# Attention and two feed-forward layers on one core: feed-forward units of one tile take two 128-blocks of the hidden layer at a time, and the order of all work is drawn anew

## The chip, the cores and the metric

The kernel runs on one core of one Trainium2 chip. The metric is the device time of one execution in microseconds, the median of several runs. TensorE has two parts in the profile, PE (matmuls) and PEld (weight loads); VectorE is DVE, ScalarE is ACT, GpSimd is POOL, and SyncE is SP, which issues the DMAs.

## The reference

Attention over 4 x 8 heads with 576 rows of 64 columns, in which each row keeps its 32 largest scores; the result, seen as 2304 tokens by 512 columns, goes through two feed-forward layers with a hidden width of 2048.

```python
scores = scale * np.matmul(q, k.transpose(0, 1, 3, 2))
kth = np.partition(scores, -top_k, axis=-1)[..., -top_k:-top_k + 1]
scores = np.where(scores >= kth, scores, -1000000000.0)
attn = np.exp(scores - np.max(scores, axis=-1, keepdims=True))
attn = attn / (np.sum(attn, axis=-1, keepdims=True) + 1e-09)
x = np.matmul(attn, v)            # then to (B * S, H * D)
x = (s * np.maximum(x @ w_in, 0.0) ** 2 + b) @ w_out      # first layer
x = np.maximum(x @ w2_in, 0.0) ** 2 @ w2_out              # second layer
```

## The kernel before

The 2304 tokens are 18 tiles of 128 (tiles 4 and 13 hold the last 64 rows of two batches). For each tile and each of its 8 heads PE makes the scores (line L599), DVE finds the 32 largest with four MAX8 and three MATCH_REPLACE8 over 576 columns (L610, L621) and writes the masked exponentials (L652 for tiles 0 to 11, L658 after that), ACT computes the exponential and a 16-bit copy (L624, L654, L661), POOL the remainder of that copy (L456), a DMA transposes both, and PE multiplies with the values (L685, 15 matmuls a head; twice as many in tiles 4 and 13). Every operand is held as a high and a low half in 16 bits, so each product takes three matmuls.

The weights come as 64-bit words. DVE, ACT and POOL convert them to 32 bits in 64 pieces (L919, L928, L935 on DVE), PE finds a scale (L980), and each piece is split into halves. W0 and W1 are the first layer's two matrices, W2 and W3 the second's.

The feed-forward work is cut into units, of one tile or of two. The first layer has 12 units of one tile (the first eleven and the last) and 3 of two; the second layer has 2 of one tile (the first and the last) and 8 of two. A unit goes through 16 blocks `f` of 128 hidden columns. For each block PE makes the hidden values in PSUM (`f_in`, 12 matmuls, L788), ACT applies ReLU (L797, out `rr`), squares it once in 16 bits (L799, `gh`) and once in 32 (L802, `gg` or `sqr`), POOL takes the difference (L807, `gl`), and PE multiplies `gh` and `gl` with the second matrix (`f_out`, 3 matmuls for each tile, L834, into the bank `pC0` or `pC1`). In a unit of two tiles all of this is 256 columns wide and the hidden values stand in the bank `pH`. In a unit of one tile it is 128 wide, and every other block uses the bank `pC1` in place of `pH` once the later weights are there:

```python
pin, pn_ = (pC[1], "pC1") if nt == 1 and h2 and rdy else (pH, "pH")
```

The order is not that of the code. `Plan.add` records each operation with its engine, a cost in us, what it reads and writes, and a priority; `Plan.order` simulates the five engines with these costs and takes, whenever an engine is free, the ready operation of lowest priority. The table `TW` adds a number to the priority, one for each group of operations (`A3.1` is tile 3, heads 2 and 3; `F04` the first layer's unit 4) and one for each step (`pe4` is `f_in`, `pe5` is `f_out`). Each engine then runs its list in that fixed order and waits at each instruction for what it needs.

Of the kernel before, what the change touches and what calls it, by code (L numbers as in the profile page):

```python
# [9 lines left out]
F16 = mybir.dt.float16  # L10
# [40 lines left out]
LASTW = 1  # L51
# [22 lines left out]
    "A0.0": -0.8, "A0.1": 19.1, "A0.2": 49.0, "A0.3": -60.0, "A1.0": 4.6, "A1.1": -6.1, "A1.2": 10.3, "A1.3": -41.3,  # L74
    "A10.0": -52.1, "A10.1": 25.4, "A10.2": 2.3, "A10.3": 0.9, "A11.0": -30.1, "A11.1": -10.9, "A11.2": 58.3,
    "A11.3": 35.8, "A12.0": 32.1, "A12.1": 45.1, "A12.2": -13.9, "A12.3": -8.8, "A13.0": -23.0, "A13.1": 59.7,
    "A13.2": 25.9, "A13.3": 2.1, "A14.0": 53.9, "A14.1": -15.9, "A14.2": 53.3, "A14.3": 57.6, "A15.0": 46.3,
    "A15.1": 1.8, "A15.2": 24.4, "A15.3": 30.8, "A16.0": -28.7, "A16.1": 46.6, "A16.2": 36.9, "A16.3": 51.2,
    "A17.0": 58.1, "A17.1": -8.9, "A17.2": 53.4, "A17.3": -50.4, "A2.0": 1.0, "A2.1": 49.3, "A2.2": -18.2,
    "A2.3": 22.0, "A3.0": 27.2, "A3.1": -35.9, "A3.2": -60.0, "A3.3": 48.1, "A4.0": 54.4, "A4.1": -60.0,  # L80
    "A4.2": -29.6, "A4.3": 35.7, "A5.0": -59.0, "A5.1": -57.6, "A5.2": -2.7, "A5.3": 23.9, "A6.0": -8.9,
    "A6.1": 58.2, "A6.2": 55.2, "A6.3": -60.0, "A7.0": -17.8, "A7.1": -22.1, "A7.2": -19.5, "A7.3": -44.5,
    "A8.0": 19.5, "A8.1": 6.1, "A8.2": -56.7, "A8.3": 60.0, "A9.0": -36.6, "A9.1": -20.3, "A9.2": 49.4,
    "A9.3": -44.4, "CS": 13.0, "E00": 14.4, "E01": 39.8, "E010": 60.2, "E011": -18.4, "E012": 9.3, "E013": -10.9,
    "E014": 1.1, "E02": 24.1, "E03": -60.0, "E04": -47.3, "E05": -52.7, "E06": -58.2, "E07": 58.5, "E08": 6.8,
# [1104 lines left out]
```

## Time and profile before

| | |
|---|---|
| three runs | 1160.61, 1156.14, 1159.86 us; median 1159.86 |
| profiled execution, first to last instruction | 1163.6 us |
| mean granted TensorE clock in it | 0.982 |
| HBM read, written | 89.65 MB, 8.91 MB |

The profiled execution is one more run of the same program, and its span is 3.7 us longer than the median of the three. A busy time in the profile is the sum of an engine's instructions; those of PE are modelled to the end of the pipeline and overlap one another, so the distance from one start to the next tells what a matmul costs.

### The profile page before, as it was taken

The page shows a single profiled execution, that of the slowest core. Times are in us where ns is not written, and L with a number is a line of the kernel's source. Part 1 is how long each engine was busy: PE and PEld are TensorE (multiplying, and loading weights), DVE is VectorE, ACT ScalarE, POOL GpSimd, SP SyncE. Part 2 cuts the span into 40 slices and gives each one's busy share as a digit, 9 for nine tenths or more (in the row PEclk, how much of TensorE's full clock was granted, in tenths as well). Part 3 has the DMA queues.
Part 4 walks back from the last instruction along what each step waited for, and adds up shares of the span by engine and source line. Part 5 has one row for each costly group of instructions (what it writes and reads, how often), then busy time and mean ns, then how long its engine had stood idle before and what let it go on. Part 6 is the DMA issues. An engine that isn't in the chain of part 4 may idle for free. (4 is left out here: it accounts for less than half of the span.)

```text
span 1163.6 us, 27825 instructions
## 1 busy us (share of the span) xinstructions
PE 1033.9 (89%) x10052; PEld 693.2 (60%) x10052; DVE 954.7 (82%) x2034; ACT 884.4 (76%) x2354; POOL 677.5 (58%) x1109
## 2 busy tenths in 40 slices
PE   1476867689989999999999999999999999999998
PEld 1232344356667667666666776666666666666665
DVE  6999999999988999999999999987999999500000
ACT  3488869879889878879987899768777686564645
POOL 4676359766667756656775577646654474452322
PEclk9988989899999999999999999999999999999999
DMA  8888974676976774687588656765376277223530
GB/s 258 243 230 199 233 193 114 181 203 138 212 124 143 151 178 84 112 189 163 98 152 183 138 104 114 172 156 118 76 178 147 53 133 181 47 64 118 172 100 29
DMA packets 338219, 171.17 MB, mean 147 GB/s; under 512 B 292512, under 2 KB 317088, under 8 KB 338080
## 3 DMA queue, kind: packets, MB, share of 16 engines
q1 hardware_dynamic: 338080, 169.39, 62.9%
q8 instruction: 78, 1.28, 0.5%
q14 instruction: 61, 0.50, 0.2%
HBM read 89.65 MB, written 8.91 MB: 85 GB/s over the span
## 5 line engine op out<-in xcount | busy, mean ns | idle before, releaser
L788 PEld LDWEIGHTS <-w 128*128 128x128 f16 x4800 | 364.6, 98 | 87.7 <-issue 23.1
L788 PE MATMUL pH<-xT,w 128*128 128x256 f16 (+1 forms) x3648 | 368.2, 251 | 12.5 <-ACT rr L797 10.5
L456 POOL TENSOR_TENSOR pn<-et,pn 128x576 f16<-128x576 f32 x144 | 185.9, 1293 | 57.6 <-ACT pn L654 24.8
L797 ACT ACTIVATE rr<-pH,rsc 128x256 f32<-128x256 f32 (+1 forms) x304 | 128.8, 424 | 109.0 <-PE pH L788 107.0
L807 POOL TENSOR_TENSOR gl<-gg,gh 128x128 f16<-128x128 f32 (+1 forms) x216 | 114.4, 530 | 141.3 <-ACT gg L802 53.0
L610 DVE MAX8 m<-wk 128x8 f32<-128x576 f32 x252 | 188.9, 749 | 1.2
L834 PE MATMUL pC<-wo,gh 128*128 128x512 f16 x576 | 171.4, 379 | 0.0
L807 POOL TENSOR_TENSOR gl<-sqr,gh 128x128 f16<-128x128 f32 (+1 forms) x184 | 100.2, 545 | 115.6 <-ACT sqr L802 53.5
L834 PE MATMUL pC<-wring,gh 128*128 128x512 f16 x544 | 161.8, 379 | 1.7 <-DMA wring<-wo 1.1
L799 ACT ACTIVATE gh<-rr 128x128 f16<-128x128 f32 (+1 forms) x400 | 139.6, 352 | 8.2 <-PE pC L834 3.0
L834 PEld LDWEIGHTS <-gh 128*128 128x128 f16 x1152 | 103.0, 98 | 68.9 <-issue 2.3
L610 DVE MAX8 m<-spare 128x8 f32<-128x576 f32 x180 | 135.0, 750 | 0.6
L624 ACT ACTIVATE et<-pS,ngm,cq 128x576 f32<-128x576 f32 x144 | 119.0, 826 | 14.7 <-DVE wk L621 3.9
L621 DVE MATCH_REPLACE8 wk<-m,wk 128x576 f32<-128x576 f32 x168 | 124.8, 743 | 0.0
L610 DVE MAX8 m<-pS 128x8 f32<-128x576 f32 x144 | 108.2, 756 | 19.1 <-PE pS L599 18.7
L685 PEld LDWEIGHTS <-pT 128*128 128x128 f16 (+1 forms) x2400 | 85.8, 102 | 44.5 <-DMA pT<-pn 29.9
L834 PE MATMUL pC<-wo,gl 128*128 128x512 f16 x288 | 109.2, 379 | 2.8 <-POOL gl L807 2.8
L685 PE MATMUL pA<-vp,pT 128*128 128x64 f16 (+1 forms) x2400 | 95.0, 196 | 16.5 <-DMA pT<-pn 15.4
L834 PE MATMUL pC<-wring,gl 128*128 128x512 f16 x272 | 103.1, 379 | 0.0
L834 PEld LDWEIGHTS <-gl 128*128 128x128 f16 x576 | 56.3, 98 | 72.9 <-POOL gl L807 5.8
L599 PE MATMUL pS<-kT,qT 128*128 128x512 f16 (+2 forms) x320 | 84.4, 298 | 12.6 <-DVE et L652 10.3
L621 DVE MATCH_REPLACE8 spare<-m,spare 128x576 f32<-128x576 f32 x120 | 89.2, 743 | 0.0
(208 smaller groups left out, 1796.4 us busy)
## 6 DMA issues: line engine op xcount, KB each, us to landing
wring<-wo SPq DMA_DIRECT2D x72, 512.0 KB, 3.9
wring<-in_moe_w_out_dram SPq DMA_DIRECT2D x18, 512.0 KB, 3.8
wring<-in_moe_w_in_dram SPq DMA_DIRECT2D x17, 512.0 KB, 4.6
xT<-in_moe_w_in_dram SPq DMA_DIRECT2D x15, 512.0 KB, 5.8
xT<-in_moe_w_out_dram SPq DMA_DIRECT2D x14, 512.0 KB, 4.3
qW<-qT SPq DMA_DIRECT2D x36, 128.0 KB, 2.4
kvraw<-in_k_dram SPq DMA_DIRECT2D x16, 256.0 KB, 3.6
kvraw<-in_v_dram SPq DMA_DIRECT2D x16, 256.0 KB, 3.2
```

Of the source, the lines that this page charges most:

```text
L456: add(pool, step, c_pool(cols * (c.stop - c.start) / n), prio, lambda c=c: nc.gpsimd.tensor_tensor(o[:, c], x[:, c], y[:, c], op=op), r=r, ...
L599: nc.tensor.matmul(s[r0:r0 + n, c0:c0 + cn_], lhsT=w[:, h, r0:r0 + n], rhs=kk[:, k0:k0 + cn_], start=(a == 0), stop=(a == 1))
L610: add(dve, "dv10", 0.67, prio, lambda src=src, rd=rd: nc.vector.max(m[:, 8 * rd:8 * rd + 8], src), r=[sn], w=[f"m{i2}_{rd}"])
L621: add(dve, "dv11", 0.735, prio, lambda src=src, rd=rd: nc.vector.match_replace(wk, m[:, 8 * rd:8 * rd + 8], src, NEG), r=[sn, f"m{i2}_{rd} ...
L624: add(act, "ac9", 0.72, prio, lambda: nc.scalar.activation(out=e, in_=s, func=ACTF.Exp, bias=ngm[i2][:, 0:1], scale=cq[q2][:, j:j + 1]), r ...
L685: nc.tensor.matmul(pA[r0:r0 + n, h, :], lhsT=pT[p3][:, a * 5 + c, r0:r0 + n], rhs=vv[:, vc, z, :], start=(c == 0 and a == 0 and z == 0), s ...
L788: nc.tensor.matmul(ps_, lhsT=win[:, f, a, kk, :], rhs=x[:, z * KD + kk, :], start=(kk == 0 and a == 0 and z == 0), stop=(kk == KD - 1 and ...
L797: add(act, "ac18", 0.14 + n / 1200.0, prio, lambda r=r, pin=pin, rs=rs: nc.scalar.activation(out=r, in_=pin[:, 0:n], func=ACTF.Relu, scale ...
L799: add(act, "ac19", 0.094 + n / 1200.0, prio, lambda r=r, hi=hi: nc.scalar.activation(out=hi, in_=r, func=ACTF.Square), r=rrn, w=ghn)
L807: add(pool, "po19", 0.12 + n * 0.0021, prio, lambda gt=gt, hi=hi, lo=lo: nc.gpsimd.tensor_tensor(lo, gt, hi, op=ALU.subtract), r=gn + ghn, ...
L834: nc.tensor.matmul(pC[tt], lhsT=src[g3][:, c], rhs=wt(a), start=(f == 0 and a == 0 and src is gh), stop=(f == KF - 1 and src is gl))
```

## The change

A unit of one tile now takes two blocks in one step (`nf = 2`). The 24 first matmuls of a step write both halves of the first 256 columns of `pH`; ReLU, both squares and the difference are one instruction each, 256 wide; six second matmuls follow. `pC1` no longer holds hidden values. Units of two tiles are computed as before. In the 14 units of one tile, 224 steps become 112, with the same matmuls. All numbers of `TW` are new, so the order of everything else changes too.

```diff
-    "A0.0": -0.8, "A0.1": 19.1, "A0.2": 49.0, "A0.3": -60.0, "A1.0": 4.6, "A1.1": -6.1, "A1.2": 10.3, "A1.3": -41.3,
+    "A0.0": -13.0, "A0.1": 32.7, "A0.2": 66.3, "A0.3": 39.0, "A1.0": -56.0, "A1.1": -21.8, "A1.2": 55.4, "A1.3": -3.9,
...
-        for f in range(KF):
+        n, nf = 256, 2 // nt
+        for f in range(0, KF, nf):
...
-            parts = "ab" if nt == 2 else "ab"[nsub[0] // 2 % 2]
-            part3 = "ab" if nt == 2 else "ab"[nsub[0] // 3 % 2]
-            if nt == 1:
-                h2, g3 = nsub[0] % 2, nsub[0] % 3
-                g1 = h2 if rdy else 0
-                nsub[0] += 1
...
-            pin, pn_ = (pC[1], "pC1") if nt == 1 and h2 and rdy else (pH, "pH")
-
-            def f_in(f=f, pin=pin):
-                ps_ = pin[:, 0:n]
-                for kk in range(KD):
-                    for a, z in ((0, 0), (0, 1), (1, 0)):
-                        nc.tensor.matmul(ps_, lhsT=win[:, f, a, kk, :], rhs=x[:, z * KD + kk, :],
-                                         start=(kk == 0 and a == 0 and z == 0),
-                                         stop=(kk == KD - 1 and a == 1))
-
-            add(pe, "pe4", 12 * max(PEN, 0.0022 + n / 2400.0), prio, f_in,
-                r=rx + [f"{wname}h{f}", f"{wname}l{f}"], w=[pn_])
+            fs = range(f, f + nf)
+
+            def f_in(fs=fs):
+                for j, ff in enumerate(fs):
+                    ps_ = pH[:, j * nt * 128:(j + 1) * nt * 128]
+                    for kk in range(KD):
+                        for a, z in ((0, 0), (0, 1), (1, 0)):
+                            nc.tensor.matmul(ps_, lhsT=win[:, ff, a, kk, :], rhs=x[:, z * KD + kk, :],
+                                             start=(kk == 0 and a == 0 and z == 0),
+                                             stop=(kk == KD - 1 and a == 1))
+
+            add(pe, "pe4", 12 * nf * (0.0022 + 128 * nt / 2400.0), prio, f_in,
+                r=rx + [f"{wname}{z}{ff}" for ff in fs for z in "hl"], w=["pH"])
...
-            add(act, "ac18", 0.14 + n / 1200.0, prio, lambda r=r, pin=pin, rs=rs: nc.scalar.activation(
-                out=r, in_=pin[:, 0:n], func=ACTF.Relu, scale=rs), r=[pn_, f"rsc{which}"], w=rrn)
+            add(act, "ac18", 0.14 + n / 1200.0, prio, lambda r=r, rs=rs: nc.scalar.activation(
+                out=r, in_=pH[:, 0:n], func=ACTF.Relu, scale=rs), r=["pH", f"rsc{which}"], w=rrn)
...
-            def f_out(f=f, g3=g3, wt=wt, o3=o3):
-                for tt in range(nt):
-                    c = slice(o3 + tt * 128, o3 + tt * 128 + 128)
+            def f_out(fs=fs, g3=g3, wt=wt):
+                for j, (ff, tt) in enumerate([(ff, tt) for ff in fs for tt in range(nt)]):
+                    c = slice(j * 128, j * 128 + 128)
                     for src, a in ((gh, 0), (gh, 1), (gl, 0)):
-                        nc.tensor.matmul(pC[tt], lhsT=src[g3][:, c], rhs=wt(a),
-                                         start=(f == 0 and a == 0 and src is gh),
-                                         stop=(f == KF - 1 and src is gl))
-
-            add(pe, "pe5", nt * 0.65, prio + 1.2, f_out, r=ghn + gln + rw,
+                        nc.tensor.matmul(pC[tt], lhsT=src[g3][:, c], rhs=wt(a, ff),
+                                         start=(ff == 0 and a == 0 and src is gh),
+                                         stop=(ff == KF - 1 and src is gl))
+
+            add(pe, "pe5", 1.3, prio + 1.2, f_out, r=[*ghn, *gln, *rw],
                 w=[f"pC{tt}" for tt in range(nt)])
```

What moves shows best on three engines. The number behind a name in the rows is that of a buffer; `pC_189` is `pC0`, `pC_190` is `pC1`, `w_67` and `w_68` are weights. In the changed file the lines stand up to 14 higher: L599 is now L598, L685 is L684, L788 is L776, L797, L799 and L802 are L784, L786 and L789, L807 is L794, L834 is L820.

First ACT, in the last unit of the second layer, a unit of one tile. Before, three instructions of 128 columns for each block, with the sources `pH` and `pC1`:

```order
L797 ACTIVATE rr_111<-pH,rsc_182 128x128
L802 ACTIVATE gg<-rr_111 128x128
L797 ACTIVATE rr_112<-pC_190,rsc_182 128x128
L802 ACTIVATE sqr<-rr_112 128x128
L799 ACTIVATE gh_114<-rr_112 128x128
L799 ACTIVATE gh_115<-rr_111 128x128
L797 ACTIVATE rr_112<-pC_190,rsc_182 128x128
L802 ACTIVATE sqr<-rr_112 128x128
L799 ACTIVATE gh_116<-rr_112 128x128
```

In the changed kernel, three of 256 columns for two blocks:

```order
L784 ACTIVATE rr_112<-pH,rsc_182 128x256
L789 ACTIVATE sqr<-rr_112 128x256
L786 ACTIVATE gh_114<-rr_112 128x256
L784 ACTIVATE rr_111<-pH,rsc_182 128x256
L789 ACTIVATE gg<-rr_111 128x256
L786 ACTIVATE gh_115<-rr_111 128x256
L784 ACTIVATE rr_112<-pH,rsc_182 128x256
L789 ACTIVATE sqr<-rr_112 128x256
L786 ACTIVATE gh_116<-rr_112 128x256
```

Nine instructions now cover six blocks where nine covered three, ReLU reads `pH` each time, and squares and ReLU alternate in a fixed turn.

Second PE, in the same unit, at the passage from a second matmul to the next first one. Before (each row with what it waits for):

```order
L834 LDWEIGHTS gh_116
L834 MATMUL pC_189<-w_67,gh_116 128x512
L834 LDWEIGHTS gh_116
L834 MATMUL pC_189<-w_67,gh_116 128x512
L834 LDWEIGHTS gl_119 [waits Pool_49]
L834 MATMUL pC_189<-w_67,gl_119 128x512
L788 LDWEIGHTS w_68
L788 MATMUL pH<-xT_110,w_68 128x128 [waits Activation_49]
```

In the changed kernel:

```order
L820 LDWEIGHTS gl_117 [waits Pool_49]
L820 MATMUL pC_189<-w_67,gl_117 128x512
L820 LDWEIGHTS gh_114
L820 MATMUL pC_189<-w_67,gh_114 128x512
L820 LDWEIGHTS gh_114
L820 MATMUL pC_189<-w_67,gh_114 128x512
L820 LDWEIGHTS gl_117
L820 MATMUL pC_189<-w_67,gl_117 128x512
L776 LDWEIGHTS w_68
L776 MATMUL pH<-xT_110,w_68 128x128 [waits Activation_49]
```

Before, the three second matmuls of one block stand between a first matmul into `pC1` and the next into `pH`. Now those of two blocks stand between one first matmul into `pH` and the next into `pH`, which waits for ACT to have read the bank.

Third POOL, during the attention of tile 1 (`pn` is the remainder of a head's probabilities, `gl` the feed-forward difference, `w_68` a piece of the second layer's first matrix being split, `knat` a block of keys). Before:

```order
L807 TENSOR_TENSOR gl_119<-gg,gh_116 128x128
L456 TENSOR_TENSOR pn_103<-et_101,pn_103 128x576
L456 TENSOR_TENSOR w_68<-w_68 128x512
L807 TENSOR_TENSOR gl_117<-gg,gh_114 128x128
L456 TENSOR_TENSOR w_68<-w_68 128x512 x2
L456 TENSOR_TENSOR pn_102<-et_100,pn_102 128x576
L807 TENSOR_TENSOR gl_118<-gg,gh_115 128x128
L456 TENSOR_TENSOR w_68<-w_68 128x512
L807 TENSOR_TENSOR gl_119<-gg,gh_116 128x128
L456 TENSOR_TENSOR knat<-kvraw_87,knat 128x8x64
L456 TENSOR_TENSOR w_68<-w_68 128x512 x2
L456 TENSOR_TENSOR pn_103<-et_101,pn_103 128x576
```

In the changed kernel, ahead of the next heads' `pn`:

```order
L455 TENSOR_TENSOR w_68<-w_68 128x512
L447 TENSOR_SCALAR wsv_177<-wsi_165 128x1
L455 TENSOR_TENSOR w_68<-w_68 128x512
L445 TENSOR_SCALAR wsc_173<-wsx_169 128x1
L455 TENSOR_TENSOR w_68<-w_68 128x512 x2
L577 TENSOR_TENSOR cq_132<-qin_197,kvinv 128x1
L455 TENSOR_TENSOR w_68<-w_68 128x512
L455 TENSOR_TENSOR w_68<-kT_78,w_68 128x512
L455 TENSOR_TENSOR w_68<-kT_79,w_68 128x512
L455 TENSOR_TENSOR pn_102<-et_100,pn_102 128x576
L455 TENSOR_TENSOR pn_103<-et_101,pn_103 128x576
```

The feed-forward differences (L807, now L794) of the first unit are gone from this place, and the pieces of the weights stand together. On PE the same shift can be counted: the 480th matmul of L685, the last product of tile 3, is row 3841 of PE's 19,884 rows before, with 63 blocks of `f_in` and 52 of `f_out` ahead of it; now it is row 2993, with 34 and 32. At the last product of tile 9 the counts are 144 blocks of one tile and 43 of two for `f_in`, 144 and 39 for `f_out` before, and 144, 41, 144 and 39 now. DVE runs the same 1,542 instructions in both.

## Rows read from the trace of the kernel before

**Rows 1.** the page, busy time of each engine, share of the span, instructions

```profile
PE 1033.9 (89%) x10052; PEld 693.2 (60%) x10052; DVE 954.7 (82%) x2034; ACT 884.4 (76%) x2354; POOL 677.5 (58%) x1109
```

**Rows 2.** windows: length, busy us PE, PEld, DVE, ACT, POOL, clock, DMA, GB/s

```profile
0.00:122.00 122.00, 63.89 (x343) 32.40 (x344) 111.33 (x213) 77.32 (x158) 71.52 (x84) 0.93 0.86 234
122.00:311.00 189.00, 150.66 (x1494) 94.14 (x1492) 185.76 (x395) 157.12 (x406) 127.19 (x189) 0.95 0.70 177
326.50:617.00 290.50, 276.97 (x3055) 193.42 (x3052) 276.77 (x591) 251.76 (x738) 192.41 (x346) 0.99 0.71 140
617.00:1015.70 398.70, 388.13 (x3845) 267.67 (x3843) 363.79 (x797) 304.82 (x787) 231.48 (x382) 1.00 0.60 128
1015.70:1163.60 147.90, 139.88 (x1140) 95.32 (x1138) 3.42 (x11) 80.50 (x226) 46.68 (x93) 1.00 0.31 95
```

**Rows 3.** the same view, PE and PEld on the attention line L685 alone

```profile
0.00:326.50 326.50, 20.28 (x480) 18.07 (x480) 0.95 0.77 200
```

**Rows 4.** the same, PE and PEld on the first-matmul line L788

```profile
0.00:326.50 326.50, 51.62 (x759) 46.31 (x760) 0.95 0.77 200
```

**Rows 5.** the same, PE and PEld on the second-matmul line L834

```profile
0.00:326.50 326.50, 40.73 (x156) 13.52 (x156) 0.95 0.77 200
```

**Rows 6.** the same, DVE on the mask line L652

```profile
0.00:311.10 311.10, 25.64 (x32) 0.95 0.76 199
```

**Rows 7.** timeline of a unit of two tiles: start, duration, engine, instructions

```profile
1125.61 1.47 PE L788 MATMUL pH<-xT,w 128*128 128x256 f16 x12
...
1126.92 0.59 PE L834 MATMUL pC<-wring,gh 128*128 128x512 f16 x2
1127.12 0.47 ACT L797 ACTIVATE rr<-pH,rsc 128x256 f32<-128x256 f32 x1 [1.38 <-PE pH L788]
...
1127.56 0.59 PE L834 MATMUL pC<-wring,gh 128*128 128x512 f16 x2
1127.62 0.42 ACT L799 ACTIVATE gh<-rr 128x256 f16<-128x256 f32 x1
...
1127.95 0.40 ACT L802 ACTIVATE sqr<-rr 128x256 f32<-128x256 f32 x1
...
1128.21 1.47 PE L788 MATMUL pH<-xT,w 128*128 128x256 f16 x12
```

**Rows 8.** timeline of a unit of one tile

```profile
1140.64 0.83 PE L788 MATMUL pC<-xT,w 128*128 128x128 f16 x12
1140.85 0.37 ACT L797 ACTIVATE rr<-pH,rsc 128x128 f32<-128x128 f32 x1
...
1141.32 0.83 PE L788 MATMUL pH<-xT,w 128*128 128x128 f16 x12
...
1141.66 0.35 ACT L797 ACTIVATE rr<-pC,rsc 128x128 f32<-128x128 f32 x1
```

**Rows 9.** groups by form: busy, mean ns, then the idle time ahead

```profile
L788 PE MATMUL pH<-xT,w 128*128 128x256 f16 x2112 | 260.5, 273 | 3.2 <-ACT rr L797 3.1
...
L788 PE MATMUL pH<-xT,w 128*128 128x128 f16 x1536 | 107.7, 220 | 9.3 <-ACT rr L797 7.4 <-DMA xT<-xn 1.7
...
L788 PE MATMUL pC<-xT,w 128*128 128x128 f16 x1152 | 80.3, 220 | 2.5 <-ACT rr L797 1.3 <-ACT xs L882 0.9
```

**Rows 10.** waits of PE from 326.5 us on: total, times, longest

```profile
PE pA L685 <- DMA pT<-pn: 11.1, 14, 2.6
PE pH L788 <- ACT rr L797: 8.6, 16, 1.0
```

**Rows 11.** windows, DVE on the conversion line L919

```profile
122.00:311.00 189.00, 18.64 (x27) 0.95 0.70 177
```

**Rows 12.** windows, DVE on the conversion line L935

```profile
122.00:311.00 189.00, 20.50 (x27) 0.95 0.70 177
```

**Rows 13.** timeline of DVE, one conversion of each of the two lines

```profile
103.26 0.42 DVE L919 TENSOR_SCALAR w<-xT 128x512 int32<-128x512 int32 x1
...
111.42 0.68 DVE L935 SCALAR_TENSOR_TENSOR w<-wring,w 128x512 int32<-128x512 int32 x1
```

More of the change, by code (lines that the diff above doesn't have):

```diff
@@ L765, in ffn @@
             g1 = h2 if rdy else 0
-            parts = "ab" if nt == 2 else "ab"[nsub[0] // 2 % 2]
-            part3 = "ab" if nt == 2 else "ab"[nsub[0] // 3 % 2]
-            if nt == 1:
-                h2, g3 = nsub[0] % 2, nsub[0] % 3
-                g1 = h2 if rdy else 0
-                nsub[0] += 1
-            o2 = 128 if parts == "b" else 0
-            o3 = 128 if part3 == "b" else 0
-            o1 = o2 if rdy else 0
-            rrn = [f"rr{h2}{z}" for z in parts]
-            ghn = [f"gh{g3}{z}" for z in part3]
@@ L778, in ffn @@
-            gln = [f"gl{g3}{z}" for z in part3]
-            gn = [(("gg", "ggb"), ("sq", "dg"))[g1]["ab".index(z)] for z in (parts if rdy or nt == 2 else "a")]
-            prio = prios[f]
-            pin, pn_ = (pC[1], "pC1") if nt == 1 and h2 and rdy else (pH, "pH")
-            def f_in(f=f, pin=pin):
-                ps_ = pin[:, 0:n]
-                for kk in range(KD):
-                    for a, z in ((0, 0), (0, 1), (1, 0)):
-                        nc.tensor.matmul(ps_, lhsT=win[:, f, a, kk, :], rhs=x[:, z * KD + kk, :],
-                                         start=(kk == 0 and a == 0 and z == 0),
-                                         stop=(kk == KD - 1 and a == 1))
@@ L792, in ffn @@
-            add(pe, "pe4", 12 * max(PEN, 0.0022 + n / 2400.0), prio, f_in,
-                r=rx + [f"{wname}h{f}", f"{wname}l{f}"], w=[pn_])
-            r, gt = rr[h2][:, o2:o2 + n], gg[g1][:, o1:o1 + n]
-            hi, lo = gh[g3][:, o3:o3 + n], gl[g3][:, o3:o3 + n]
+            rrn = [f"rr{h2}{z}" for z in "ab"]
+            ghn = [f"gh{g3}{z}" for z in "ab"]
+            gln = [f"gl{g3}{z}" for z in "ab"]
+            gn = [("gg", "ggb"), ("sq", "dg")][g1]
+            prio = prios[f]
+            fs = range(f, f + nf)
@@ L807, in ffn @@
             add(pool, "po19", 0.12 + n * 0.0021, prio, lambda gt=gt, hi=hi, lo=lo: nc.gpsimd.tensor_tensor(
-                lo, gt, hi, op=ALU.subtract), r=gn + ghn, w=gln)
+                lo, gt, hi, op=ALU.subtract), r=[*gn, *ghn], w=gln)
             if which == 0:
-                rw = [f"wo1h{f}", f"wo1l{f}"]
-                wt = lambda a, f=f: wo1[:, f, a, :]
-            else:
-                if u >= len(units[1]) - LASTW:
-                    late = w1[:, f - f % 2:f - f % 2 + 2].rearrange("p f a k c -> p f a (k c)")
-                    rw = [f"w1{z}{f - f % 2 + i}" for z in "hl" for i in range(2)]
-                    if f % 2 == 0 and u == len(units[1]) - LASTW:
-                        add(sp, "sp15", 0.47, prio - LWP, lambda late=late, f=f: dma(late, wo2[f // 2]),
-                            r=[f"wo2_{f}", f"wo2_{f + 1}"], w=rw, lat=1.46)
-                    wt = lambda a, f=f, late=late: late[:, f % 2, a, :]
-                elif f % 2 == 0:
+                rw = [f"wo1{z}{ff}" for ff in fs for z in "hl"]
+                wt = lambda a, ff: wo1[:, ff, a, :]
+            elif u >= len(units[1]) - LASTW:
+                late = w1[:, f - f % 2:f - f % 2 + 2].rearrange("p f a k c -> p f a (k c)")
+                rw = [f"w1{z}{f - f % 2 + i}" for z in "hl" for i in range(2)]
+                if f % 2 == 0 and u == len(units[1]) - LASTW:
+                    add(sp, "sp15", 0.47, prio - LWP, lambda late=late, f=f: dma(late, wo2[f // 2]),
+                        r=[f"wo2_{f}", f"wo2_{f + 1}"], w=rw, lat=1.46)
+                wt = lambda a, ff, late=late: late[:, ff % 2, a, :]
+            else:
+                if f % 2 == 0:
                     ri = nring[0] % NWR
```

10 lines of the change are left out of this document (4 added, 6 removed), and 75 rows, old and new, of the table TW.

## The prediction

> **What bounds the kernel now.** I read the busy times first. PE is busy 1033.9 of 1163.6 us and DVE 954.7 [rows 1]. Such shares are averages, so the next view is the busy time by stretch [rows 2]; the reader should subtract each busy time from the length of its stretch. Up to 311 us the bound is DVE: it stands still 10.7 us of the first 122 (the start) and 3.2 us of the 189 that follow, while PE stands still 58 and 38 us. From 326.5 to 617 us both are nearly full (PE idle 13.5 us, DVE 13.7 us). From 617 to 1015.7 PE idles 10.6 us and DVE 34.9 us. Behind that DVE is done, and PE alone works for the last 147.9 us with 8.0 us idle. So the time is PE's work plus PE's idle time, nearly all of which lies ahead of 326.5 us, where DVE sets the pace with the conversion of the weights and the top-k search. ACT and POOL are nowhere full: 251.8 and 192.4 of the 290.5 us.
>
> Next come the places in the program. The line of the attention product has 480 matmuls by 326.5 us [rows 3], at 15 a head: 32 heads, which are tiles 0 to 3. I call this moment A. The stretches of [rows 2] that end at 617.0 and 1015.7 us end, by the same count, with the last products of tiles 9 and 17. By A PE has run 760 weight loads of the first feed-forward matmul, 12 a block: 63 blocks and a few matmuls of the next [rows 4]. It has run 156 of the second, 3 a block: 52 blocks [rows 5]. DVE wrote the mask of the 32nd head by 311.1 us [rows 6], so PE finished A 15.4 us behind DVE.
>
> Last, the timeline for prices. In a unit of two tiles the first matmul's 12 passes begin at 1125.61, the second's two parts at 1126.92 and 1127.56, and the next first matmul at 1128.21 [rows 7]: 0.64 us for 128 columns of the second, 2.60 us a step, and no gap. In a unit of one tile the 12 passes of one block begin 0.68 us apart [rows 8].
>
> **The change part by part.** PE's matmuls are the same in number and shape. 112 steps of 24 first and 6 second passes replace 224 of 12 and 3, at the same 0.68 and 0.64 us a block. What PE does in total is therefore unchanged: 0.
>
> ACT ran one block in 0.81 us (ReLU at 1140.85, the next block's at 1141.66 [rows 8]); one 256-wide set takes 0.50 to the first square, 0.33 to the next and 0.40 for it, 1.23 us [rows 7]. That saves 2 x 0.81 - 1.23 = 0.39 us a step, 44 us over 112 steps. ACT is not the bound, so this is worth only what PE waits for ReLU. Those waits are 7.4 + 1.3 us in units of one tile and 3.1 us in units of two [rows 9]; most of them, 8.6 us on pH, fall behind A [rows 10]. The units of two tiles already work as the new code does, one bank and a 256-wide ReLU: 3.1 us in 176 steps, or 2 us in 112. I take 4 us less waiting behind A, with bounds from 0 to 8.6. POOL's fewer instructions I cost at nothing: POOL is busy two thirds of the time behind A. If its cover were gone, a late difference would show as a wait of the second matmul.
>
> The order is the larger part. Before A's last attention product, PE's new order holds 34 first blocks and 32 second ones, where 63 and 52 stood. By the last product of tile 9 both orders have done the same but for two 256-wide first matmuls that the new one still owes. So 29 x 0.68 + 20 x 0.64 = 32.5 us of PE's work moves from ahead of A, where PE had idle time, to behind it, where PE is full. Taken alone: **+32.5 us**.
>
> Against it stands that A comes earlier. A waits for DVE, whose operations are the same. In 122 to 311 us DVE can win its 3.2 us of idle time, and what the conversions lose. They took 18.64 us for 27 and 20.50 us for 27 [rows 11, 12], where an undisturbed one takes 0.42 and 0.68 [rows 13]: 39.1 - 29.7 = 9.4 us too long, some of it with POOL's feed-forward differences in between, which are now later. Bounds 0 and 12.6 us; I take 4, since POOL's own weight work fills the freed room (the order shows it). The 15.4 us by which PE trailed DVE at A can shrink too. Copy, difference, transpose and product must follow the mask in any case, so I take half, 8 us, bounds 0 and 8. Together **-12 us** (0 to -20.6).
>
> Behind A the added work can fill PE's idle time up to tile 9, 13.5 us [rows 2]. More can't be filled: PE's 277.0 + 32.5 = 309.5 us are then the bound there, above DVE's 276.8. I take all of it, **-13.5 us**, because a late PE finds the transposed probabilities landed (the waits for them are 11.1 us behind A [rows 10]); the other end is a third of it, -4.5, where waits stay as they are. The ReLU waits give **-4 us**.
>
> At the end, one unit of one tile remains in both orders. With two blocks a step the last second matmul has one step ahead of it to hide ReLU, squares and difference instead of several queued blocks: **+1 us**, bounds 0 and 2.
>
> Sum: 32.5 - 12 - 13.5 - 4 + 1 = +4. The profiled execution goes from 1163.6 to 1167.6 us. It lies 3.7 us above the median of the three runs, 1159.86, so the median goes to about 1164.
>
> **The rivals.** *Faster: the early stretch shortens.* If the deferred feed-forward work takes POOL out of DVE's way, A comes 18 us earlier (10 on DVE, 8 on PE), all 13.5 us are filled and 8 us of ReLU waits go: 32.5 - 18 - 13.5 - 8 = -7, a median of 1153. For it: conversions of 1 us and more among those of 0.42. Against it: POOL's freed places hold weight differences. It decides once A comes before 305 us; with every bound at its best it would be 1148.
>
> *Slower: one bank.* In units of one tile, two banks took turns (pH and pC); now PE's next first matmul waits until ReLU has read pH. Uncovered, that is 1127.59 - 1126.92 = 0.67 us a step [rows 7], 75 us in 112 steps. In the row it costs nothing, since the two second matmuls lie in between. Where ACT is busy with an exponential, the cover may fail. If one step in four is uncovered, about +19 us comes on top: 1184. It decides from one step in nine. Against it stands that the units of two tiles do so already [rows 9].
>
> The Trainium skill ("PSUM — Partial Sum Buffer", section "PSUM bank collisions raise a hardware error") states that the hardware does not arbitrate two engines on one bank, so a program must keep them apart. By this alone each step would pay its wait; the trace shows the wait hidden behind the second matmul, and the sum goes by the trace.
>
> *Slower: the moved work is not absorbed.* A comes 10 us earlier, only 5 us of idle time is filled and no ReLU wait goes: 32.5 - 10 - 5 + 1 = +18.5, a median of 1178. For it: behind A, PE and DVE are both full, each instruction waits in a fixed order, and a late score product holds DVE up as well. The granted clock adds to it: it was 0.93 to 0.95 ahead of 311 us and about 1.00 behind [rows 2], and a PE with 32.5 us less to do in 122 to 311 us (118 of 189) may be granted less. Two hundredths of 118 us are 2 us.
>
> The Trainium skill ("TensorE: Matmul & The Clock Gate", section "What's actually happening") says that the throttled clock is the default and that activity releases it. The rows agree: the clock is lowest where PE idles most.
>
> *Nothing changes.* PE catches up by tile 9 behind a DVE that sets the pace, and 1160 remains; this is within the first case's range.
>
> **How the numbers follow.** The case of the sum, with the median from 1156 to 1172, gets 0.44; early shortening 0.26; one bank 0.10; not absorbed 0.20. About 0.5%, 1154.1 to 1165.7, is what three runs between 1156.1 and 1160.6 can tell from no change. The sum's case lies 0.33 within, 0.09 above, 0.02 below. So faster 0.28, same 0.33, slower 0.39. The likeliest time stays that of the sum. The range takes in the early case down to 1147 and the unabsorbed case up to 1186.
>
> **What would show it.** Right: 32 heads' products end near 314 us with 34 first blocks done; from there to tile 9's last product some 306 to 311 us, with PE idle under 8 us; ReLU waits of PE under 6 us in all; ACT's busy time down by 44 us or more. Wrong: A before 305 us, or PE idle of 13 us or more between A and tile 9, or ReLU waits over 10 us. A stretch behind tile 17's last product much different from 147.9 us would mean that the order moved more than I counted.

## The result and the profile after

The changed kernel takes 1176.47 us (median; 1173.38 to 1181.38) against 1160.23 of the kernel before in the same comparison: 1.0142 times as long, interval 1.0105 to 1.018, so 16.2 us slower. The profiled execution spans 1179.6 us, against 1163.6. The page's first line and its row of the granted clock:

```profile
PE 1049.9 (89%) x10052; PEld 701.6 (59%) x10052; DVE 953.1 (81%) x2034; ACT 855.9 (73%) x2018; POOL 660.1 (56%) x997
...
PEclk9968985679999999999999999999998999999999
```

ACT lost 28.5 us of busy time, not the 44 forecast, and POOL 17.4; DVE is as before [rows 1]. (A busy time counts stretches in which two instructions of an engine overlap once; it is not the plain sum that the section on the time before calls it.) PE has the same matmuls. Some 425 of them moved behind A, the last product of tile 3; its busy time ahead of A fell by only 15.4 us (228.9 to 213.5), and behind A it rose by 31.5. Ahead of A the mean granted clock was 0.83 instead of 0.95, and there the 128x512 matmuls of 32 bits that split the weights took from 592 to 1223 ns each.

The windows by stretch answer to [rows 2]. The third, fourth and fifth begin and end at the same events as there: the last products of tiles 3, 9 and 17.

```profile
0.00:122.00 122.00, 64.71 (x312) 31.18 (x313) 110.46 (x213) 75.99 (x156) 73.67 (x83) 0.85 0.89 245
122.00:311.00 189.00, 142.04 (x1206) 84.07 (x1205) 184.33 (x399) 140.71 (x300) 113.27 (x152) 0.82 0.61 158
317.70:630.30 312.60, 305.17 (x3453) 217.55 (x3454) 285.45 (x609) 257.11 (x657) 197.64 (x323) 0.99 0.67 148
630.30:1033.30 403.00, 388.85 (x3844) 267.04 (x3843) 362.90 (x792) 297.99 (x714) 225.97 (x356) 0.99 0.57 124
1033.30:1179.60 146.30, 142.43 (x1165) 97.51 (x1162) 3.42 (x11) 78.67 (x181) 45.33 (x79) 0.99 0.31 96
```

In the second row PE runs 288 matmuls fewer than before (1206 against 1494) and the clock is 0.82 instead of 0.95. In the third the matmuls come back (3453 against 3055) and the stretch is 312.6 us long instead of 290.5. By stretch: up to A 317.7 instead of 326.5 (-8.8), A to tile 9 +22.1, to tile 17 +4.3, behind it -1.6; sum +16.0.

The same view up to A, for the attention line L684, the first matmul L776 and the second L820, answers to [rows 3 to 5]:

```profile
0.00:317.80 317.80, 23.92 (x480) 21.92 (x480) 0.83 0.72 191
...
0.00:317.80 317.80, 26.37 (x408) 24.50 (x408) 0.83 0.72 191
...
0.00:317.80 317.80, 23.00 (x96) 8.79 (x96) 0.83 0.72 191
```

408 by 12 and 96 by 3: 34 first and 32 second blocks ahead of A, where 63 and 52 were. The last mask ahead of A, by which PE's lateness behind DVE is read, is done by 310.8 us, as [rows 6] has it by 311.1:

```profile
0.00:310.80 310.80, 25.81 (x32) 0.83 0.72 193
```

What PE waited for from A on (total, times, longest) answers to [rows 10]. One more line of the kernel before:

```profile
PE pC L788 <- ACT rr L797: 1.3, 2, 0.7
```

The changed kernel:

```profile
PE pA L684 <- DMA pT<-pn: 12.8, 13, 3.1
PE pH L776 <- DMA xT<-xn: 4.2, 2, 4.0
PE pH L776 <- ACT rr L784: 2.1, 3, 0.9
```

The waits for ReLU fell from 9.9 us (8.6 and 1.3) to 2.1. Those for the transposed probabilities did not fall, and one of 4.0 us for transposed tokens is new. PE's timeline shows it (in brackets the idle time ahead and what ended it):

```profile
895.22 0.61 PE L684 MATMUL pA<-vp,pT 128*128 128x64 f16 x15 [0.88 <-DMA pT<-pn]
899.85 2.72 PE L776 MATMUL pH<-xT,w 128*128 128x256 f16 x12 [4.01 <-DMA xT<-xn]
902.36 0.63 PE L598 MATMUL pS<-kT,qT 128*128 128x512 f16 x1
```

PE stood still for 4.01 us until the transposed tokens of a unit had landed. The next twelve passes took 2.5 us to the next start, where 1.3 is usual [rows 7]. The window of these passes shows why:

```profile
899.80:902.40 2.60, 2.55 (x13) 1.82 (x13) 2.43 (x6) 0.67 (x1) 0.88 (x1) 0.50 0.49 148
```

The granted clock is 0.50, the lower level of 1.2 GHz.

### The profile page after: what moved, and what is told of

Read it like the earlier page. It is cut to its first block, busy times and chain, and to the rows that moved or that the text cites. A ratio compares the mean times of both kernels' runs of the same rounds, so it can differ in the third digit from the quotient of the medians.

```text
span 1179.6 us, 27340 instructions
## 1 busy us (share of the span) xinstructions
PE 1049.9 (89%) x10052; PEld 701.6 (59%) x10052; DVE 953.1 (81%) x2034; ACT 855.9 (73%) x2018; POOL 660.1 (56%) x997
## 5 line engine op out<-in xcount | busy, mean ns | idle before, releaser
L776 PE MATMUL pH<-xT,w 128*128 128x128 f16 (+1 forms) x4800 | 431.2, 244 | 8.2 <-DMA xT<-xn 4.2
L776 PEld LDWEIGHTS <-w 128*128 128x128 f16 x4800 | 360.3, 98 | 68.2 <-issue 9.6
L784 ACT ACTIVATE rr<-pH,rsc 128x256 f32<-128x256 f32 x288 | 135.5, 471 | 128.6 <-PE pH L776 124.9
L794 POOL TENSOR_TENSOR gl<-gg,gh 128x256 f16<-128x256 f32 x152 | 102.2, 673 | 128.8 <-ACT gh L786 96.3
L820 PE MATMUL pC<-wo,gh 128*128 128x512 f16 x576 | 172.1, 380 | 0.5 <-ACT xs L868 0.3
L794 POOL TENSOR_TENSOR gl<-sqr,gh 128x256 f16<-128x256 f32 x136 | 91.5, 673 | 128.4 <-ACT gh L786 96.5
L820 PE MATMUL pC<-wring,gh 128*128 128x512 f16 x544 | 161.8, 379 | 0.0
L820 PEld LDWEIGHTS <-gh 128*128 128x128 f16 x1152 | 104.9, 98 | 74.7 <-issue 1.4
L786 ACT ACTIVATE gh<-rr 128x256 f16<-128x256 f32 x288 | 117.8, 409 | 11.6 <-PE pC L820 6.4
L684 PEld LDWEIGHTS <-pT 128*128 128x128 f16 (+1 forms) x2400 | 89.4, 104 | 47.5 <-DMA pT<-pn 26.2
L684 PE MATMUL pA<-vp,pT 128*128 128x64 f16 (+1 forms) x2400 | 97.5, 198 | 20.3 <-DMA pT<-pn 20.1
L820 PE MATMUL pC<-wo,gl 128*128 128x512 f16 x288 | 109.4, 380 | 0.0
L820 PE MATMUL pC<-wring,gl 128*128 128x512 f16 x272 | 103.1, 379 | 0.9 <-POOL gl L794 0.8
L598 PE MATMUL pS<-kT,qT 128*128 128x512 f16 (+2 forms) x320 | 86.2, 306 | 15.8 <-DVE et L651 12.7
L820 PEld LDWEIGHTS <-gl 128*128 128x128 f16 x576 | 56.4, 98 | 71.6 <-POOL gl L794 4.0
```

Of the source, the lines that this page charges most:

```text
L598: nc.tensor.matmul(s[r0:r0 + n, c0:c0 + cn_], lhsT=w[:, h, r0:r0 + n], rhs=kk[:, k0:k0 + cn_], start=(a == 0), stop=(a == 1))
L684: nc.tensor.matmul(pA[r0:r0 + n, h, :], lhsT=pT[p3][:, a * 5 + c, r0:r0 + n], rhs=vv[:, vc, z, :], start=(c == 0 and a == 0 and z == 0), s ...
L776: nc.tensor.matmul(ps_, lhsT=win[:, ff, a, kk, :], rhs=x[:, z * KD + kk, :], start=(kk == 0 and a == 0 and z == 0), stop=(kk == KD - 1 and ...
L784: add(act, "ac18", 0.14 + n / 1200.0, prio, lambda r=r, rs=rs: nc.scalar.activation(out=r, in_=pH[:, 0:n], func=ACTF.Relu, scale=rs), r=[" ...
L786: add(act, "ac19", 0.094 + n / 1200.0, prio, lambda r=r, hi=hi: nc.scalar.activation(out=hi, in_=r, func=ACTF.Square), r=rrn, w=ghn)
L794: add(pool, "po19", 0.12 + n * 0.0021, prio, lambda gt=gt, hi=hi, lo=lo: nc.gpsimd.tensor_tensor(lo, gt, hi, op=ALU.subtract), r=[*gn, *gh ...
```

## The experiments

Three theories were put to the test. **T1, the shared half:** the changed code itself sends the feed-forward work behind A. The 128 x 128 diagonal matrix with which PE splits W3 lies in the right half of the square's buffer (the expectations below say W2 and W3, but W2's pieces are split by ACT and POOL, without it: `SPLIT = ('P', 'P', 'O', 'P')`):

```python
dgs = [gg[0][:, 0:128], gg[0][:, 128:256]]
```

In the kernel before, early one-block steps squared into the left half alone (`parts if rdy or nt == 2 else "a"`). The 256-wide square writes both halves, so it may not run until the last piece of W3 is split. **T2, the table:** the new numbers of `TW` move the work, as the prediction assumed. **T3, the wide step itself:** one bank and the longer chain cost the time.

The trace shows the moment on which T1 rests. In each pair stand the first squares (count, duration, first and last start, up to 275 us) and some of the splits with the diagonal. The kernel before, L802 and L957:

```profile
L802 ACT ACTIVATE gg<-rr x31: 292/300/313, 157.6 to 274.3; 128x128 f32<-128x128 f32 x31
...
L957 PE MATMUL pC<-vp,gg x10: 592/676/1222, 215.4 to 279.7; 128*128 128x512 f32 x10
```

The changed kernel, L789 and L943:

```profile
L789 ACT ACTIVATE gg<-rr x5: 399/417/421, 266.8 to 274.6; 128x256 f32<-128x256 f32 x5
...
L943 PE MATMUL pC<-vp,gg x10: 592/697/1222, 204.0 to 265.4; 128*128 128x512 f32 x10
```

Before, squares ran from 157.6 us on, ahead of these splits and among them. Now the first comes at 266.8, 1.4 us behind the start of the last split. All kernels below fall on one side or the other. Where the plan has the early square write the half that holds the diagonal (dep_only, step_only, after_jitter, after_refit), the first square starts 2.1 to 3.4 us behind the start of the last split; in all others it starts 110 us or more ahead of it.

The table sums up all kernels. "Blocks" are the first and second 128-blocks ahead of A. "Plan's end" is the time at which `Plan.order`, by the costs written in the kernel, expects the last operation; it is no time of the chip. The ratio is to the kernel before in the same comparison (medians 1158.92, 1158.53 and 1159.0 us for the first, second and third four).

| kernel | blocks | plan's end | span | median | ratio and interval |
|---|---|---|---|---|---|
| before | 63 / 52 | 1136.1 | 1163.6 | 1160.23 | |
| after | 34 / 32 | 1151.6 | 1179.6 | 1176.47 | 1.0142 (1.0105 to 1.018) |
| own_diag | 58 / 48 | 1153.2 | 1174.1 | 1175.82 | 1.0147 (1.0124 to 1.0171) |
| dep_only | 27 / 24 | 1187.3 | 1206.3 | 1208.63 | 1.044 (1.041 to 1.0471) |
| step_only | 34 / 30 | 1175.1 | 1197.8 | 1198.17 | 1.0348 (1.0325 to 1.0371) |
| table_only | 56 / 46 | 1158.5 | 1172.7 | 1173.63 | 1.0139 (1.0117 to 1.016) |
| own_diag_old_table | 60 / 52 | 1156.1 | 1181.9 | 1181.77 | 1.0199 (1.0167 to 1.0231) |
| own_diag_mix | 58 / 50 | 1151.1 | 1174.9 | 1176.23 | 1.0157 (1.0131 to 1.0184) |
| jitter | 59 / 49 | 1172.1 | 1191.8 | 1193.65 | 1.0305 (1.0283 to 1.0327) |
| after_jitter | 30 / 26 | 1174.3 | 1197.7 | 1201.51 | 1.038 (1.0352 to 1.0407) |
| before_refit | 58 / 50 | 1130.6 | 1153.4 | 1152.18 | 0.9956 (0.9936 to 0.9976) |
| after_refit | 42 / 36 | 1135.8 | 1160.3 | 1161.03 | 1.0012 (0.9998 to 1.0027) |
| own_diag_refit | 56 / 46 | 1122.9 | 1145.5 | 1146.4 | 0.9893 (0.9877 to 0.991) |
| own_diag_refit2 | 54 / 44 | 1125.1 | 1145.2 | 1147.06 | 0.9906 (0.9889 to 0.9923) |

**own_diag**: the changed kernel with the diagonal in a tile of its own; three groups of one-column tiles are merged to make room.

```diff
-    dgs = [gg[0][:, 0:128], gg[0][:, 128:256]]
+    dgx = T([128, 128], F32, "dgx")
+    dgs = [gg[0][:, 0:128], dgx]
...
-            add(pe, "pe6", 1.08, prio, f_sub, r=[f"dgs{d}", ("gg", "ggb")[d], "minus"] + on + hn, w=pdn)
+            add(pe, "pe6", 1.08, prio, f_sub, r=[f"dgs{d}", ("gg", "dgx")[d], "minus"] + on + hn, w=pdn)
```

> The changed kernel with one thing more: the diagonal matrix that splits W2 and W3 has 128 columns of its own and no longer lies in the right half of gg. By the order, 58 first blocks and 48 second ones then stand ahead of the last product of tile 3, where the changed kernel has 34 and 32. Theory 1 (the 256-wide square needs that half, so the units of one tile wait until W3 is split; that is what moved the work): back to 1155 to 1166 us, tile 3's products end near 320 us and those of tile 9 near 617. Theory 2 (the new table of priorities moved the work): 1172 us or more. Theory 3 (the wide step itself costs: one bank, longer chain): 1172 us or more, with PE waiting for ReLU.

The blocks came back, 58 and 48, with the table unchanged; the time did not, as T2 and T3 had it. The products of tiles 3 and 9 end at 326.8 and 633.8 us, not near 320 and 617. So the step moves the work, and something else holds the time.

**dep_only**: the kernel before, in which the early one-block square is merely declared to write both halves.

```diff
-            gn = [(("gg", "ggb"), ("sq", "dg"))[g1]["ab".index(z)] for z in (parts if rdy or nt == 2 else "a")]
+            gn = [(("gg", "ggb"), ("sq", "dg"))[g1]["ab".index(z)] for z in (parts if rdy or nt == 2 else "ab")]
```

> The kernel before, with its steps of one block and its table; only the square of a one-block step is declared to write both halves of gg, so the planner keeps it behind the splitting of W2 and W3. By the order, 27 first and 24 second blocks stand ahead of tile 3's last product (63 and 52 before). Theory 1: 36 x 0.68 + 28 x 0.64 = 42 us of PE's work moved, of which half to three quarters comes back as time: 1178 to 1192 us. Theories 2 and 3: 1156 to 1164 us, since neither the table nor the width of a step is changed.

No instruction is added or widened, and 36 first and 28 second blocks move behind A. That this one declaration does it is the plainest proof of T1's place; the 49.7 us are more than the 36 x 0.68 + 28 x 0.64 = 42.4 us of moved work.

**step_only** (the changed code with the table of before) and **table_only** (the code of before with the new table). The diff is that of step_only, of whose table one line stands; table_only is its reverse on the other code:

```diff
-    "A0.0": -13.0, "A0.1": 32.7, "A0.2": 66.3, "A0.3": 39.0, "A1.0": -56.0, "A1.1": -21.8, "A1.2": 55.4, "A1.3": -3.9,
+    "A0.0": -0.8, "A0.1": 19.1, "A0.2": 49.0, "A0.3": -60.0, "A1.0": 4.6, "A1.1": -6.1, "A1.2": 10.3, "A1.3": -41.3,
...
```

> The changed kernel with the table of priorities of the kernel before: two blocks a step, old table. By the order, 34 first and 30 second blocks stand ahead of tile 3's last product. Theory 1: slower, 1170 to 1184 us. Theory 2: 1156 to 1164 us. Theory 3: slower, 1170 to 1184 us, with waits of PE for ReLU of more than 10 us.

> The kernel before with the table of priorities of the changed kernel: one block a step, new table. By the order, 56 first and 46 second blocks stand ahead of tile 3's last product. Theory 1: near the kernel before, 1156 to 1168 us. Theory 2: like the changed kernel, 1172 to 1182 us. Theory 3: 1156 to 1164 us.

The blocks follow the code and not the table: 34 and 30 with the new code, 56 and 46 with the old. That settles T2 as to where the work goes. But table_only is 14.7 us slower, within T2's range, although only 7 and 6 blocks moved; and in all four runs the time lies above T1's range. In step_only PE waited 13.5 us for ReLU behind A, over 10 as T3 expected:

```profile
PE pH L777 <- ACT rr L785: 13.5, 19, 2.0
```

A table seems to fit only the code that it was drawn for. The next four runs went after that.

**own_diag_old_table** and **own_diag_mix** give own_diag other tables: that of before, and one with the numbers of before for weights, tiles 0 to 3 and steps and the new ones for later groups. **jitter** and **after_jitter** leave the code of before and after as it is and move every number of the table by up to 2 at random:

```diff
-    "A0.0": -0.8, "A0.1": 19.1, "A0.2": 49.0, "A0.3": -60.0, "A1.0": 4.6, "A1.1": -6.1, "A1.2": 10.3, "A1.3": -41.3,
+    "A0.0": -2.3, "A0.1": 20.5, "A0.2": 50.1, "A0.3": -61.0, "A1.0": 4.6, "A1.1": -6.3,
+    "A1.2": 10.9, "A1.3": -40.1, "A10.0": -53.7, "A10.1": 23.5, "A10.2": 3.6, "A10.3": 0.6,
```

> Two blocks a step, the diagonal matrix in its own 128 columns, and the table of the kernel before: as step_only (1198 us), but without the shared half of gg. By the order, 60 first and 52 second blocks stand ahead of tile 3's last product (34 and 30 in step_only, 63 and 52 before). Theory 1 (the shared half moves the work): 1160 to 1175 us, at least 23 us under step_only; PE's work ahead of that product within 6 us of the kernel before. Theory 3 (the wide step itself costs): 1190 us or more. A table that was drawn for other steps may cost some 10 us, as in table_only.

> As own_diag, with a mixed table: the values of the kernel before for the weights, the tiles 0 to 3 and the steps, those of the changed kernel for all later groups. 58 first and 50 second blocks ahead of tile 3's last product. Theory 1 with a table that fits poorly: 1160 to 1176 us. If own_diag was slow because the new table delays tile 0 (its mask ended 9 us later than before), this one has tile 3's last product within 3 us of the kernel before and lies at least 5 us under own_diag (1176).

> The kernel before with every value of its table moved by up to 2 at random, nothing else. This measures what a table is worth that fits its kernel. If the orders of these programs are worth 10 us and more by themselves, it takes 1165 to 1180 us; if a table matters only by what it moves past tile 3, it stays within 1156 to 1166 us (59 and 49 blocks ahead of tile 3's last product, 63 and 52 before).

> The changed kernel with every value of its table moved by up to 2 at random. 30 first and 26 second blocks ahead of tile 3's last product (34 and 32). If the changed kernel's 1176 us is what the moved work costs under any table, 1172 to 1186 us; if its table is fitted to the moved work and gains by that, like step_only and dep_only: 1188 to 1205 us.

own_diag_old_table lies between the ranges of T1 and T3, and 16.4 us under step_only instead of 23 or more. own_diag_mix lies just above its range: A comes at 324.6 us, within 3 us of the kernel before, but the time is that of own_diag, so a late tile 0 was not what held own_diag up. jitter lies above both of its ranges, after_jitter in the one for a fitted table.

The numbers of before lie between -60 and 60.2; random changes of up to 2 cost 35.1 us there, and 25.0 in the changed kernel (1201.51 to 1176.47), more than the change itself. Each engine runs its list in order, so an instruction whose input is late holds up all behind it. The longest wait of DVE from 800 to 890 us in jitter is such a one:

```profile
DVE et L670 <- ACT et L636: 8.8, 1, 8.8
```

In the kernel before no wait of DVE in these 90 us was longer than 0.9. The blocks of own_diag came back with every table (58 to 60 and 48 to 52), and none of its three tables brought the median below 1175 us. So a comparison in which the code changes and the table stays tells little of the code. The last four runs give each code a table drawn for it: random changes of the numbers, kept where the plan's own end falls. **before_refit**, **after_refit** and **own_diag_refit** are the codes of before, of after and of own_diag; **own_diag_refit2** is own_diag again, from another starting table. Only `TW` differs, here by a line of before_refit:

```diff
-    "A0.0": -0.8, "A0.1": 19.1, "A0.2": 49.0, "A0.3": -60.0, "A1.0": 4.6, "A1.1": -6.1, "A1.2": 10.3, "A1.3": -41.3,
+    "A0.0": -10.2, "A0.1": 7.0, "A0.2": -3.8, "A0.3": 11.4, "A1.0": -0.9, "A1.1": 18.9, "A1.2": -67.2, "A1.3": -4.7,
...
```

> The code of the kernel before with a table drawn for it anew: random changes of the numbers, kept where the plan's own end time falls (from 1136.1 to 1130.6 us). In the ten kernels run so far the profiled span was 14 to 28 us above the plan's end. If the table's fit is what sets the differences, 1150 to 1162, within 0.8% of before; 58 first blocks and 50 second ones stand ahead of A.

> The code of the changed kernel, shared half included, with a table drawn anew for it in the same way and with as much effort (plan's end from 1151.6 to 1135.8 us). 42 first and 36 second blocks stand ahead of A. If the shared half moves work that can't be wholly won back: 1157 to 1168, slower than the refitted kernel before by some 5 us and than the one with its own diagonal by 10 or more. If the table alone made the change slow: no slower than the refitted kernel before, about 1155.

> The changed code with the diagonal in a tile of its own, table drawn anew with the same effort from the table of before (plan's end from 1155.7 to 1122.9 us). 56 first and 46 second blocks stand ahead of A. If the shared half is what costs and the wide step is itself good: 1142 to 1154, faster than before and than both other refitted kernels. If the wide step itself costs (one bank, a chain of ReLU, squares and difference): no faster than the refitted kernel before, whatever the table.

> The same code as the run before it, with another table, drawn anew from the changed kernel's table (plan's end from 1153.2 to 1125.1 us); 54 first and 44 second blocks stand ahead of A. If a table's fit by the plan carries over to the chip, it comes out within 6 us of the run before it: 1144 to 1156. If the fit is to the plan alone, the two may differ by 10 us or more and lie above 1160.

All four times lie inside the ranges expected; for after_refit and own_diag_refit these are the ones that go with the shared half as the cause, with a wide step that is good in itself. The two tables for own_diag, from different starts, give medians 0.7 us apart, so the comparison of refitted kernels should carry a few us. For the other two codes one table each was drawn, so their spread is not known. The windows up to A and then by stretch as above, of before_refit:

```profile
0.00:320.50 320.50, 223.60 (x1940) 135.18 (x1941) 301.17 (x627) 242.55 (x591) 208.73 (x281) 0.94 0.78 203
320.50:611.80 291.30, 280.21 (x3131) 196.88 (x3129) 279.36 (x597) 255.80 (x752) 196.71 (x355) 1.00 0.66 143
611.80:1007.90 396.10, 388.30 (x3860) 268.12 (x3858) 364.90 (x802) 307.12 (x788) 230.07 (x380) 1.00 0.58 127
1007.90:1153.40 145.50, 138.31 (x1128) 94.22 (x1126) 3.42 (x11) 79.68 (x226) 46.61 (x93) 1.00 0.31 97
```

Of after_refit:

```profile
0.00:328.50 328.50, 212.44 (x1705) 123.07 (x1706) 310.73 (x627) 229.57 (x485) 196.80 (x250) 0.89 0.74 187
328.50:625.00 296.50, 294.35 (x3340) 209.41 (x3338) 284.43 (x601) 250.98 (x642) 193.68 (x313) 1.00 0.71 151
625.00:1020.50 395.50, 391.61 (x3893) 270.78 (x3891) 361.72 (x797) 296.07 (x719) 227.82 (x358) 1.00 0.59 129
1020.50:1160.30 139.80, 135.97 (x1124) 93.46 (x1120) 3.42 (x11) 71.07 (x175) 43.20 (x77) 1.00 0.32 100
```

Of own_diag_refit:

```profile
0.00:323.00 323.00, 216.81 (x1910) 133.43 (x1911) 308.20 (x630) 232.31 (x501) 206.27 (x254) 0.94 0.76 199
323.00:610.30 287.30, 284.07 (x3174) 200.66 (x3172) 278.34 (x596) 245.13 (x630) 189.73 (x310) 1.00 0.72 150
610.30:1003.00 392.70, 385.85 (x3836) 265.71 (x3834) 363.92 (x798) 295.91 (x713) 226.01 (x356) 1.00 0.57 127
1003.00:1145.50 142.50, 138.57 (x1142) 95.20 (x1138) 3.42 (x11) 72.06 (x178) 43.92 (x77) 1.00 0.32 99
```

The first squares and some of the splits of own_diag_refit, L793 and L947:

```profile
L793 ACT ACTIVATE gg<-rr x15: 399/414/434, 162.8 to 274.5; 128x256 f32<-128x256 f32 x15
...
L947 PE MATMUL pC<-vp,dgx x10: 592/620/1200, 208.7 to 286.6; 128*128 128x512 f32 x10
```

With a diagonal of its own the squares start at 162.8 us, ahead of these splits and then among them. With the shared half the first square of after_refit comes at 264.4 us, behind the last split's start at 262.0, and the kernel runs 205 matmuls fewer ahead of A (1705 against 1910) and 166 more from there to tile 9, a stretch that PE fills to within 2.2 us (294.35 of 296.5); there is no idle time left in it to hide more work in. 14 first and 10 second blocks fewer ahead of A are 14 x 0.68 + 10 x 0.64 = 15.9 us of PE's work, and the median is 14.6 us longer. That the two are so near is partly chance. By stretch the profiled executions differ by 5.5 us up to A, 9.2 to tile 9, 2.8 to tile 17 and -2.7 behind it, so about 9 us lie where the moved work went; why A comes 5.5 us later, with DVE busy for 310.7 us of that time instead of 308.2, stays open.

The wide step, own_diag_refit against before_refit, gains 5.8 us (5.1 with the second table; 7.9 between the profiled executions), each code with its own table. PE's waits from A on show where the time was gained. Of before_refit:

```profile
PE pA L684 <- DMA pT<-pn: 10.8, 12, 1.9
PE pH L787 <- ACT rr L796: 8.0, 16, 1.0
```

Of own_diag_refit:

```profile
PE pA L685 <- DMA pT<-pn: 4.6, 5, 2.3
...
PE pH L780 <- ACT rr L788: 1.3, 3, 0.8
```

The waits for ReLU fell by 6.7 us, as they did in the changed kernel, and those for the transposed probabilities by 6.2. How much of this is the step's and how much the table's is not shown: with tables not drawn for it, the same wide step waited for ReLU longer than the kernel before (9.9 us), 13.5 us in step_only, 12.7 in own_diag_old_table and 11.9 in own_diag_mix. T3 is refuted in this sense: with a table of its own the wide step costs nothing over the narrow one. own_diag_refit beats both kernels: 12.6 us less than before.

## Why the prediction came out as it did

The forecast was 1164 with a range up to 1186; the median is 1176.5. Of its cases the rival "the moved work is not absorbed" (1178) describes the time best, while the sum missed it by 12 us. That 1178 came so near is partly luck: this rival has no gain from ReLU, which gave 7.8 us, and no loss from tile 9 to 17, which cost 4.3. By its steps, in the profiled execution (sum +4, measured +16.0):

- **The moved work, +32.5.** The counts were right, 34 and 32 blocks, and PE's busy time behind A rose by 31.5 us. The cause was not: the prediction put it down to the new order ("The order is the larger part"). dep_only, step_only and own_diag show that it is the step, through the shared half. Had the prediction asked which buffers the 256-wide square writes and who else reads them, it would have found this in the code.
- **A earlier, -12: measured -8.8.** PE's lateness behind DVE's last mask shrank as forecast, from 15.4 to 7.0 us (A at 317.7, mask at 310.7). DVE gave 0.4 instead of 4.
- **The idle time filled, -13.5, and ReLU, -4.** The stretch from A to tile 9 should have grown by 15.0 us and grew by 22.1. This is the step that failed: PE's idle time there fell from 13.5 to 7.4 us, so 6.1 us were filled, near the rival's 5. The reason given, that a late PE finds the probabilities landed, was wrong here: those waits rose from 11.1 to 12.8 us. The ReLU waits are part of this idle time: in the stretch they fell from 4.9 us (3.6 on pH, 1.3 on pC1) to 0.9, so the sum, which took them beside the 13.5, counted these twice. Over all stretches behind A they gave 7.8 us, not 4. The rival "one bank" did not come about here: of the steps of one-tile units behind A the profile shows a single one that waited for ReLU, for 0.9 us. Its 0.67 us is no fixed price, though; step_only's waits show that one bank can cost more under another table.
- **From tile 9 to 17, nothing: measured +4.3**, about as much as the single wait at 899.85 us and the slow matmuls behind it. The prediction compared counts at tile 9 and took the rest for equal.
- **The end, +1: measured -1.6**, with 25 matmuls more than before in that stretch: PE's idle time there fell from 8.0 to 3.9 us, 2.3 of it waits for ReLU. The term had the wrong sign.

So +3.2, +7.1, +4.3 and -2.6 against the sum make the 12 us. ACT's saving was mis-sized too, 28.5 us instead of 44, but no term rested on it. Two of the prediction's side sums do not come out: with every bound at its best the early case gives 1150, not 1148, and one bank gives 1183, not 1184. Two of its signs of being right, PE idle under 8 us up to tile 9 (7.4) and ReLU waits under 6 us (2.1), came true although the sum missed, so they could not tell the cases apart.

The refitted kernels divide the change's 16.2 us otherwise: the wide step -5.8, the shared half +14.6, and the rest, 7.4, is put down to a table that fits its code less well. That rest is what a new table wins more in the changed code, 15.4 us (1176.47 to 1161.03), than in that of before, 8.1 (1160.23 to 1152.18, or 6.8 from the 1159.0 measured beside it). The division holds to a few us at best, by which such tables may differ. Why the changed kernel's table fits less well stays open, and so does how much lower any of the codes could go.

The clock fell much further ahead of 311 us than the two hundredths taken, from 0.93 and 0.95 to 0.85 and 0.82, and A still came earlier. The Trainium skill ("TensorE: Matmul & The Clock Gate", section "What's actually happening") has activity release the throttle; the trace agrees from 122 to 311 us, where the clock fell and 288 matmuls went missing. In the first 122 us, with 31 fewer, the cause of the fall is not shown.

## What to carry to other kernels

Before a step is made wider, look at every buffer that it now writes in full and at who else keeps something there: a 128 x 128 scratch matrix in an unused half cost 15 us, and a 64 KB tile of its own turned a loss of 8.9 us into a gain of 5.8, each code with a table drawn for it. When a hand-fitted static order goes with the code, neither the old nor the new table gives a fair comparison of the code; draw a table for each with equal effort and compare those. Where the bound engine has work moved to a stretch that it already fills, do not count on idle time to take it up: here 32.5, 42.4 and 15.9 us of moved work went with 16.2, 49.7 and 14.6 us of time, and in the first of these A came 8.8 us earlier.

## What was not expected

- The order's sensitivity. jitter runs the instructions of the kernel before, and the first eight experiments lie between 1173.6 and 1208.6 us. The kernel's own plan told them apart to within some 14 us: over all fourteen kernels the profiled span was 14.2 to 28.0 us above the plan's end, which itself ranges over 64 us (1122.9 to 1187.3).
- The clock ahead of A cost nothing visible. own_diag_refit and own_diag_refit2, the same code with two tables, had a mean granted clock of 0.94 and 0.87 ahead of A, and A came at 323.0 and 321.9 us. The four executions of own_diag_refit, with one table, point the same way: at mean clocks of 0.982, 0.963, 0.964 and 0.982 over the whole span they took 1147.23, 1145.74, 1145.44 and 1147.06 us. The window of own_diag_refit2:

```profile
0.00:321.90 321.90, 214.54 (x1868) 132.61 (x1868) 304.32 (x626) 230.32 (x495) 198.25 (x252) 0.87 0.76 196
```

There DVE is busy for 304.3 of 321.9 us and PE for 214.5; so there the lower of PE's two levels, 1.2 GHz, seems to use up idle time of its own. Behind A the lower level does cost, as the row at 899.8 us shows.
